# Attention block on one core: seven single PSUM banks for scores and maxima, every exp over one bank

## The chip, the cores and the metric

One core of a Trainium2 chip runs the whole block in one launch. The metric is device time in microseconds (us). Engines: PE (TensorE) multiplies, ACT (ScalarE) does exp, Abs and copies, DVE (VectorE) reduces and adds, POOL (GpSimd) splits and copies in SBUF, SP (SyncE) issues most DMAs. PSUM, where PE writes, has eight banks of 512 fp32 columns on 128 partitions.

## The reference, cut to what matters

```python
    def _A_ref(x, wqkv, wo):
        B, S, D = x.shape
        H = 32; Dh = D // H
        qkv = (lambda x, *d: x.transpose(*d))((x @ wqkv).reshape(B, S, 3, H, Dh), 2, 0, 3, 1, 4)
        q, k, v = qkv[0], qkv[1], qkv[2]
        scale = Dh ** -0.5
        scores = jnp.einsum("bhqd,bhkd->bhqk", q, k) * scale
        p = _softmax(scores, axis=-1)
        o = jnp.einsum("bhqk,bhkd->bhqd", p, v)
        return (lambda x, *d: x.transpose(*d))(o, 0, 2, 1, 3).reshape(B, S, D) @ wo
...
    h = x + _A_ref(_layernorm(x, axis=-1), A_wqkv, A_wo)
    h2 = h + _B_ref(_layernorm(h, axis=-1), B_w_in, B_w_sp, B_b_sp, B_w_out)
```

There are S = 2048 tokens of D = 512, and 32 heads of 16. The change lies within the attention, between the projections of q, k and v and the product with `wo`. `_B_ref`, a gated block with a 2048 x 2048 product over the sequence, is untouched.

## The kernel before

All of q, k and v are in scratch memory in DRAM after the first stage. The attention then goes over eight groups of four heads (`hg`), four blocks of 512 queries (`qb`) and 16 blocks of 128 keys (`kb`). One (hg, qb, kb) is a **unit**: for each of four heads the scores of 128 keys against 512 queries, their exp, and the product of the exps with v. There are 512 units, and a **turn** of the loop (`n` goes by two) handles two of them.

The four heads of a group are told apart by t (0 or 1) and p (0 or 1). Heads with t = 0 have their q and k on partitions 0 to 49, those with t = 1 on partitions 64 to 113 (`RG = 64`), that is on the lower and on the upper rows of PE. A score product has 50 rows: three 16-row parts of q and k and two rows that subtract the maximum of the query's scores, so that exp needs no bias. Those maxima have to be known before: for a **max pair** (128 queries, the two heads t = 0 and t = 1 of one p) `max_pair` (L217) makes eight products of 48 rows with 512 columns each:

- `M`, four of them: t = 1, 512 keys each, then DVE's maximum over the bank (L240).
- `m`, two: t = 0, keys 1024 to 2047, likewise.
- `v` and `u`: t = 0, the first 1024 keys through half sums and half differences; ACT takes the absolute value of `v`'s bank into SBUF (L245), DVE adds `u`'s bank to it and takes the maximum in one instruction (L249).

After eight max pairs `N` joins their maxima (`end`, L251), and `T` turns them and writes them by DMA into q's rows (`max_rows`, L275). The max pairs run 11 turns (`LEAD`) ahead of the units that need them. A turn has one max pair; of the eight turns of a (hg, qb), the first two share two.

The order of PE, ACT, DVE and SP is written out by hand (`tc.manual_schedule`): `play` (L749) goes through a list of tokens and issues each token's instructions on all engines. In the old lists, `S` is one score product; two of them (first t = 0, then t = 1) fill a tile `s` of two banks, and the second issues an exp over both, 1024 columns (L715), into a tile `pt`. `M1` is a max product into bank m1 with its reader on DVE or ACT. `h` is half of the `pv` products of the last turn's second unit (256 columns), `V` all of those of this turn's first unit (`weigh`, L720); each has four products of 32 output rows, for the four heads, that accumulate in the bank `pv` over 16 units. `G` copies that bank out (`gather`).

PSUM in this stage: three banks m0 to m2 for maxima, two tiles `s` of two banks in rotation, and `pv`. A product into a bank waits for the last reader of that bank; an exp waits for its products and for the `pv` products that read its `pt` tile six tiles before; `pv` products wait for the exps.

ORDER is played in most turns, START in the first, and the two lists of FIRST_TWO in the first two turns of each further (hg, qb). Once no maxima are left (the last eleven turns), the maxima's banks go to a third `s` tile and to `h`, and other code (`play_four` and the lines after it) takes over.

Of the kernel before, what the change touches and what calls it, by code (L numbers as in the profile page):

```python
# [18 lines left out]
P = 128  # L19
# [24 lines left out]
START = "S S m1 M0 S S h M2 v1 S S m0 S S M2 u1 V M0".split()  # L44
# [14 lines left out]
def block_kernel(ctx: ExitStack, tc: tile.TileContext, x, wqkv, wo, w_in, w_sp4, b_sp, w_out, out):  # L59
# [622 lines left out]
    with ExitStack() as at:  # L682
# [9 lines left out]
        def score(*unit):  # L692
            first, second = scores_of(*unit)
            first()
            return second()

        def scores_of(hg, qb, kb, p):

            q, k = qst[hg * NQ + qb], kst[hg % 2]
            turn[0] += len(later)
            pool = later[0] if later and turn[0] % 3 == 2 else ps_s
            s = pool.tile([P, 2, 512], F32, name="s")

            def product(t):
                r = slice(RG * t, RG * t + KM)
                nc.tensor.matmul(s[:, t, :], k[r, p, kb * P:(kb + 1) * P], q[r, p, :],  # L709
                                 start=True, stop=True)  # L710

            def second():
                product(1)
                t = pp.tile([P, 2, 512], F32, name="pt")
                nc.scalar.activation(t, s, AF.Exp, scale=DH ** -0.5)  # L715
                return t

            return lambda: product(0), second

        def weigh(hg, qb, kb, pts, cols=slice(0, 512)):  # L720

            if kb == 0:
                pv[0] = ps_v.tile([P, 512], F32, name="pv")
            for j in range(4):
                c = (4 * kb + j) * VW
                nc.tensor.matmul(pv[0][32 * j:32 * j + 32, cols], vst[hg % 2][:, c:c + 32],  # L726
                                 pts[j % 2][:, j // 2, cols], start=kb == 0,
                                 stop=kb == NB - 1 and cols.stop == 512)

        def gather(hg, qb, pool=sm):  # L730

# [17 lines left out]
        def play(order, prev, unit):  # L749

            hg, qb, *kbs = unit
            ending = pending[:]
            pending[:] = ends
            ends.clear()
            halves = [slice(0, 256), slice(256, 512)]
            opened, pts = [], []
            for x in order:
                if x == "S":
                    if opened:
                        pts.append(opened.pop()())  # L760
                    else:
                        k, p = divmod(len(pts), 2)
                        first, second = scores_of(hg, qb, kbs[k], p)
                        first()
                        opened.append(second)
                elif x == "h":
                    cols = halves.pop(0)
                    if prev is not None:
                        weigh(*prev, cols)
                    elif halves:  # L770

                        pv[0] = ps_v.tile([P, 512], F32, name="pv")
                        for j in range(4):
                            nc.tensor.matmul(pv[0][32 * j:32 * j + 32, :], vst[0][:, :32],
                                             vst[0][:, :512], start=True, stop=True)
                elif x == "V":
                    weigh(hg, qb, kbs[0], pts[:2])
                elif x == "G":
                    gather(*prev[:2])
                elif x == "N":  # L780
                    if ending:
                        ending.pop()()
                elif x == "T":
                    if turned:
                        max_rows()
                    elif kbs[0] == 6 and sums_:
                        invert()
                else:
                    steps_of[x[0]].pop(0)(int(x[1:]))
            assert not ending and len(pts) == 4  # L790
            played.append(pts[2:])

        def play_four(at, prev):

            waiting, opened = [prev], []
            for x in FOUR:
                if x == "S":
                    if opened:
                        pts = waiting[-1][-1]
                        pts.append(opened.pop()())  # L800
                    else:
                        if waiting[-1] is prev or len(waiting[-1][-1]) == 2:
                            waiting.append((*at.pop(0), []))
                        unit = waiting[-1]
                        first, second = scores_of(*unit[:3], len(unit[-1]))
                        first()
                        opened.append(second)
                elif x == "V":
                    unit = waiting.pop(0)
                    weigh(*unit)  # L810
                    if unit[2] == NB - 1:
                        gather(*unit[:2])
                else:
                    more_h(1)
            return waiting.pop()

        played, pending = [], []
        steps_of = {kind: [] for kind in "Mmvu"}
# [40 lines left out]
        prev, turn, later = None, [2], []  # L859
        with tc.manual_schedule(engines={E.PE, E.Activation, E.DVE, E.SP}):  # L860
            for n in range(0, len(units), 2):
                (hg, qb, kb), (_, _, kb1) = units[n:n + 2]
                if hg + 1 < HG and n % 64 < 24 and n % 4 == 0:
                    load_k(hg + 1, [n % 64 // 4])
                if hg + 1 < HG and n % 64 < 12 and n % 4 == 2:
# [9 lines left out]
                    m += 1  # L875
                if not steps and not later:
                    maxima.close()
                    later.append(attn.enter_context(
                        tc.tile_pool(name="ps_l", bufs=1, space=PSUM, side="right")))
                if steps:  # L880
                    play(START if not n else FIRST_TWO[place] if place < 2 < n else ORDER, prev, (hg, qb, kb, kb1))
                    pts1 = played.pop()
                elif n % 4 == 0:
                    if n == 504:
                        load_o(h_rows[3])
                    prev = play_four(units[n:n + 4], prev)
                elif n < 492:
                    if pending:
                        pending.pop()()
                    pts = [score(hg, qb, kb, 0), score(hg, qb, kb, 1)]  # L890
                    weigh(*prev)
                    pts1 = [score(hg, qb, kb1, 0), score(hg, qb, kb1, 1)]
                    more_h(4)
                    weigh(hg, qb, kb, pts)
                    if turned:
                        max_rows()
                if steps or n == 490:
                    prev = (hg, qb, kb1, pts1)
# [8 lines left out]
            weigh(*prev)  # L907
            gather(*prev[:2], e2)
    attn.close()


# [520 lines left out]
```

## Time and profile before

| | us |
|---|---|
| median of 3 runs | 1850.19 (1849.8 to 1851.92) |
| profiled execution, first to last instruction (span) | 1848.2 |
| PE busy | 1840.2 |
| DVE busy | 1519.0 |
| ACT busy | 1363.4 |
| POOL busy | 225.7 |
| attention, first exp to last exp's start | 165.5 to 1393.4 |

The profiled execution has no time of its own beside its span; the median of the runs is 2.0 us above that span. A row of a group reads: line, engine, operation, output and inputs, shapes, count, then busy time and mean duration of one in ns, then the idle time of the engine just before these instructions and what ended it. PE's weight loads are listed apart (PEld): a product that must wait waits in its load. In the time line a row is one or more like instructions in a row on one engine: start, time to the end of the last, and in brackets how long the engine was idle before. In the windows a row gives, for a stretch, the busy time and count of PE, PEld, DVE, ACT and POOL, then PE's granted clock and the DMA share and rate.

### The profile page before, as it was taken

The numbers are of one execution on the slowest core, as the hardware profiler recorded it, in microseconds if no ns is written. First come the engines' busy times: TensorE is split into PE (matmuls) and PEld (weight loads), VectorE is DVE, ScalarE is ACT, GpSimd is POOL, SyncE is SP. The second block draws the span as 40 slices with busy tenths as digits, with TensorE's granted clock in tenths as the row PEclk, the third lists the DMA queues.
The fourth block names the chain that finished last, engine by engine and source line by source line (L and its number), as shares of the span: only waits on it lengthen the run. The fifth ranks groups of instructions, "written<-read, shape, count | busy, mean of one in ns | idle before, by whom it ended". The sixth has DMA issues, their size and how long they took to land.

```text
span 1848.2 us, 35986 instructions
## 1 busy us (share of the span) xinstructions
PE 1840.2 (100%) x13362; PEld 1028.3 (56%) x13362; DVE 1519.0 (82%) x3030; ACT 1363.4 (74%) x1696; POOL 225.7 (12%) x305
## 2 busy tenths in 40 slices
PE   9999999999999999999999999999999999999999
PEld 6875334433334333344333334343437889999998
DVE  6578999999999999999999999999936766877664
ACT  3325999999999999999999999999995444434221
POOL 2241000011010100000000000000001756001111
PEclk9999999999999999999999999999999999999999
DMA  6778111221120111022011012100124555768662
GB/s 195 198 193 193 42 25 31 55 47 29 39 57 18 53 39 25 17 50 39 14 39 38 19 30 49 25 14 14 31 55 124 165 162 170 224 189 272 200 195 91
DMA packets 148759, 160.15 MB, mean 87 GB/s; under 512 B 63096, under 2 KB 93320, under 8 KB 147240
## 3 DMA queue, kind: packets, MB, share of 16 engines
q1 hardware_dynamic: 143800, 146.44, 29.5%
q10 hardware_dynamic: 4752, 11.41, 1.6%
q8 instruction: 105, 1.72, 0.4%
q14 instruction: 70, 0.57, 0.1%
q0 software_dynamic: 32, 0.01, 0.0%
HBM read 101.26 MB, written 55.61 MB: 85 GB/s over the span
## 4 chain that ended last, share of the span: by engine, by line
PE 99%; DVE 0%; ACT 0%; issue 0%; DVEq 0%; ACTq 0%
PE pv L726 29%; PE m L235 22%; PE s L709 15%; PE acc L106 6%; PE acc L108 5%; PE acc L107 5%; PE g L108 4%; PE g L107 4%; PE g L106 4%; PE acc L644 2%; PE tp L1300 1%; PE acc L1321 0%; PE tp L996 0%; PE tp L389 0%; PE h L644 0%; PE acc L465 0%
## 5 line engine op out<-in xcount | busy, mean ns | idle before, releaser
L240 DVE TENSOR_REDUCE mx<-m 128x1 f32<-128x512 f32 x1508 | 948.5, 684 | 94.1 <-PE m L235 64.1
L715 ACT ACTIVATE pt<-s 128x1024 f32<-128x1024 f32 x1024 | 1012.5, 1024 | 12.6 <-PE m L235 6.6
L726 PE MATMUL pv<-pt,vst 128*32 128x256 f32 (+1 forms) x6048 | 590.5, 466 | 0.0
L235 PE MATMUL m<-kst,qst 48*128 48x512 f32 x1508 | 578.0, 468 | 0.1
L709 PE MATMUL s<-qst,kst 50*128 50x512 f32 x2048 | 568.1, 427 | 0.6 <-ACT pt L715 0.5
L235 PEld LDWEIGHTS m<-kst,qst 48*128 48x128 f32 x1508 | 236.7, 184 | 342.6 <-DVE mx L240 302.8
L709 PEld LDWEIGHTS s<-qst,kst 50*128 50x128 f32 x2048 | 273.5, 184 | 136.4 <-ACT pt L715 92.2
L726 PEld LDWEIGHTS pv<-pt,vst 128*32 128x32 f32 x6048 | 122.8, 108 | 227.5 <-issue 215.4
L235 PE MATMUL m<-uvs,qst 48*128 48x512 f32 x497 | 227.7, 458 | 0.0
L245 ACT ACTIVATE ab<-m 128x512 f32<-128x512 f32 x248 | 148.4, 598 | 76.5 <-PE m L235 76.4
L249 DVE CUSTOM_DVE_ANT_0 ab<-m,ab 128x512 f32<-128x512 f32 x249 | 169.4, 680 | 10.6 <-ACT pt L715 9.9
L100 POOL CAST mparts<-nm 128x16 fp32r<-128x16 f32 x32 | 6.3, 198 | 881.7 <-DVE nm L253 881.7
L235 PEld LDWEIGHTS m<-uvs,qst 48*128 48x128 f32 x497 | 90.8, 183 | 37.5 <-DVE mx L240 37.5
L936 ACT ACTIVATE ws<-a 128x512 fp32r<-128x512 f32 x80 | 45.7, 621 | 48.7 <-PE g L108 23.9
L1015 ACT ACTIVATE z<-acc 128x464 f32<-128x464 f32 (+2 forms) x64 | 27.6, 456 | 67.1 <-PE acc L108 67.1
L106 PE MATMUL acc<-wi,hT 128*128 128x464 f32 (+2 forms) x196 | 72.8, 371 | 0.0
L108 PE MATMUL acc<-wi,hT 128*128 128x464 f32 (+2 forms) x196 | 71.8, 366 | 0.0
L107 PE MATMUL acc<-wi,hT 128*128 128x464 f32 (+2 forms) x196 | 71.6, 365 | 0.0
L937 DVE TENSOR_TENSOR ws<-a,ws 128x512 fp32r<-128x512 f32 x80 | 56.3, 746 | 11.6 <-ACT ws L936 11.4
L98 ACT ACTIVATE part<-acc 128x512 fp32r<-128x512 f32 x32 | 19.1, 597 | 60.9 <-PE acc L108 51.6
L106 PE MATMUL g<-b,ws 128*128 128x344 f32 x192 | 62.6, 326 | 0.0
L936 ACT ACTIVATE ws<-s 128x512 fp32r<-128x512 f32 x32 | 19.5, 631 | 57.7 <-DVE s L956 57.7
(201 smaller groups left out, 2156.9 us busy)
## 6 DMA issues: line engine op xcount, KB each, us to landing
a<-in_w_sp SPq DMA_DIRECT2D x80, 256.0 KB
qst<-q_scr SPq DMA_DIRECT2D x192, 64.0 KB
z_scr<-z ACTq DMA_DIRECT2D x32, 344.0 KB
kst<-k_scr SPq DMA_DIRECT2D x42, 256.0 KB
k_scr<-part SPq DMA_DIRECT2D x16, 512.0 KB
q_scr<-part SPq DMA_DIRECT2D x16, 512.0 KB
z<-z_scr SPq DMA_DIRECT2D x14, 344.0 KB
b<-z_scr SPq DMA_DIRECT2D x24, 172.0 KB
```

Source lines behind the costliest of these rows:

```text
L106: nc.tensor.matmul(ps, lh, rh, start=first, stop=False)
L107: nc.tensor.matmul(ps, lh, rl, start=False, stop=False)
L108: nc.tensor.matmul(ps, ll, rh, start=False, stop=last)
L235: nc.tensor.matmul(acc, q[r, p, c], keys[r, p], start=True, stop=True)
L240: nc.vector.reduce_max(at(t, e if t else e - 1), acc, axis=AX.X)
L245: nc.scalar.activation(ab[0], acc, AF.Abs)
L249: nc.vector.tensor_tensor_reduce(ab[0], acc, ab[0], 0.5, LOW, ALU.add, ALU.max, at(0, 0))
L709: nc.tensor.matmul(s[:, t, :], k[r, p, kb * P:(kb + 1) * P], q[r, p, :], start=True, stop=True)
L715: nc.scalar.activation(t, s, AF.Exp, scale=DH ** -0.5)
L726: nc.tensor.matmul(pv[0][32 * j:32 * j + 32, cols], vst[hg % 2][:, c:c + 32], pts[j % 2][:, j // 2, cols], start=kb == 0, stop=kb == NB - ...
L936: nc.scalar.activation(hi, src, AF.Copy)
L937: (nc.gpsimd if el == "pool" else nc.vector).tensor_sub(lo, src, hi.bitcast(F32))
```

## The change

Scores and maxima now share seven single banks, numbered 0 to 6: 0 to 2 are m0 to m2 as before, 3 to 6 are four single tiles s0 to s3 in place of the two tiles of two banks. Any score product and any max product may name any of them. Each score token names its head row and its bank (`Sa5`: t = 0, bank 5; `Sb1`: t = 1, bank 1) and issues its own exp over that one bank, 512 columns, into a quarter of a tile `pt` that holds a whole unit. `pt` has three buffers of four banks' size in place of six of two. `weigh` takes the four heads in the order in which their exps were issued. `h` and `V` take the oldest unit that waits. The lists are new; the two of FIRST_TWO are joined into one over two turns. After the last maximum the code uses exps over two banks as before, from a pool that is opened then.

```diff
+MB = 3
-ORDER = "v2 S S M1 N S h m0 S m1 M2 S S h S M0 u1 T S V M0".split()
+ORDER = "Sa5 M6 m3 M2 v4 Sb1 h Sb6 u0 M5 Sa4 h Sb2 m3 Sb6 Sa1 N M4 Sa0 V T".split()
...
-FIRST_TWO = ["v2 S S M1 S h S m2 M0 h G M1 S S m2 S m0 S V".split(),
-             "u2 S S M1 m0 S S h h v2 M1 S S M0 S S M2 u1 V M0".split()]
+FIRST_TWO = ("M5 Sa3 M2 Sa4 Sb1 Sb0 m6 h Sa4 M2 v3 m5 Sb1 M6 h u2 G Sa5 Sb3 m0 Sb4 M1 Sa6 V "
+             "v0 M2 Sa3 M5 u1 Sb4 h h Sa2 Sb5 m6 M3 Sb1 Sa0 V").split()
...
-        pp = at.enter_context(tc.tile_pool(name="pp", bufs=6))
+        pp = at.enter_context(tc.tile_pool(name="pp", bufs=3))
...
-        ps_s = at.enter_context(tc.tile_pool(name="ps_s", bufs=2, space=PSUM))
+        singles = at.enter_context(ExitStack())
+        ps_s = singles.enter_context(tc.tile_pool(name="ps_s", bufs=1, space=PSUM))
...
+        def new_pt():
+            return pp.tile([P, 4, 512], F32, name="pt")
...
+        def exp(out, scores):
+            nc.scalar.activation(out, scores, AF.Exp, scale=DH ** -0.5)
...
-            for j in range(4):
+            for t, p in sorted(places, key=places.get):
+                j = 2 * t + p
                 c = (4 * kb + j) * VW
                 nc.tensor.matmul(pv[0][32 * j:32 * j + 32, cols], vst[hg % 2][:, c:c + 32],
-                                 pts[j % 2][:, j // 2, cols], start=kb == 0,
+                                 pt[:, places[t, p], cols], start=kb == 0,
                                  stop=kb == NB - 1 and cols.stop == 512)
...
-                if x == "S":
-                    if opened:
-                        pts.append(opened.pop()())
-                    else:
-                        k, p = divmod(len(pts), 2)
-                        first, second = scores_of(hg, qb, kbs[k], p)
-                        first()
-                        opened.append(second)
+                if x[0] == "S":
+                    if not open_:
+                        open_.extend([units.pop(0), new_pt(), {}])
+                    unit, pt, places = open_
+                    t = "ab".index(x[1])
+                    p = sum(u == t for u, _ in places)
+                    out = bank(int(x[2:]))
+                    product(out, *unit, t, p)
+                    exp(pt[:, len(places), :], out)
+                    places[t, p] = len(places)
+                    if len(places) == 4:
+                        waiting.append([tuple(open_), 0])
+                        open_.clear()
...
+        for b in range(4):
+            more[MB + b] = lambda b=b: ps_s.tile([P, 512], F32, name=f"s{b}")
...
                     maxima.close()
+                    singles.close()
+                    doubles.append(at.enter_context(tc.tile_pool(name="ps_d", bufs=2, space=PSUM)))
```

How PE's instructions move, in an ORDER turn in the middle of the attention. These are PE's rows of before from a turn's first product to the one ahead of the second h; `m` with `kst` or `uvs` are max products, `s` score products, and the brackets name the engines whose semaphores a product waits for.

```order
L235 MATMUL m_9029<-uvs_1734,qst 128x512
L709 MATMUL s<-qst,kst_1733 128x512 [waits Activation_49]
L709 MATMUL s<-qst,kst_1733 128x512
L235 MATMUL m_9038<-kst_1733,qst 128x512 [waits DVE_49]
L709 MATMUL s<-qst,kst_1733 128x512 [waits Activation_49]
L726 MATMUL pv<-pt,vst_104 32x256 x4
L235 MATMUL m_9047<-kst_1733,qst 128x512 [waits DVE_49]
L709 MATMUL s<-qst,kst_1733 128x512
L235 MATMUL m_9053<-kst_1733,qst 128x512 [waits DVE_49]
L235 MATMUL m_9056<-kst_1733,qst 128x512 [waits Activation_49]
L709 MATMUL s<-qst,kst_1733 128x512 [waits Activation_49]
L709 MATMUL s<-qst,kst_1733 128x512
```

And PE's rows of the changed kernel from a turn's first product, Sa5, to the one ahead of the second h. L700 is a score product and L236 a max product; the name of the output says which pool the bank is from.

```order
L700 MATMUL s_9726<-qst,kst_1733 128x512 [waits DVE_49]
L236 MATMUL s_9729<-kst_1733,qst 128x512 [waits Activation_49]
L236 MATMUL s_9732<-kst_1733,qst 128x512 [waits DVE_49]
L236 MATMUL m_9735<-kst_1733,qst 128x512
L236 MATMUL s_9738<-uvs_1734,qst 128x512 [waits DVE_49]
L700 MATMUL m_9742<-qst,kst_1733 128x512 [waits Activation_49]
L726 MATMUL pv<-pt,vst_104 32x256 x3
L726 MATMUL pv<-pt,vst_104 32x256 [waits Activation_49]
L700 MATMUL s_9749<-qst,kst_1733 128x512 [waits DVE_49]
L236 MATMUL m_9752<-uvs_1734,qst 128x512
L236 MATMUL s_9755<-kst_1733,qst 128x512 [waits Activation_49]
L700 MATMUL s_9758<-qst,kst_1733 128x512 [waits Activation_49]
```

Both kinds now write into both pools' banks, and products of either kind wait for DVE and for ACT, whichever read the bank last. The second h follows on two pairs instead of three behind the first.

On ACT, these are two turns of before: an Abs and four exps over two banks.

```order
L245 ACTIVATE ab<-m_8966 128x512 [waits DVE_49,PE_49]
L715 ACTIVATE pt<-s 128x1024 [waits PE_49,Activation_49] x4
L245 ACTIVATE ab<-m_9029 128x512 [waits DVE_49,PE_49]
L715 ACTIVATE pt<-s 128x1024 [waits PE_49,Activation_49] x4
L245 ACTIVATE ab<-m_9088 128x512 [waits DVE_49,PE_49]
```

And one turn of the changed kernel, from the exp of Sa5 to that of the next turn's Sa5:

```order
L704 ACTIVATE pt<-s_16317 128x512 [waits PE_49,Activation_49]
L246 ACTIVATE ab<-s_16329 128x512 [waits PE_49]
L704 ACTIVATE pt<-m_16333 128x512 [waits PE_49]
L704 ACTIVATE pt<-s_16340 128x512 [waits PE_49]
L704 ACTIVATE pt<-s_16349 128x512 [waits PE_49]
L704 ACTIVATE pt<-m_16357 128x512 [waits PE_49,Activation_49]
L704 ACTIVATE pt<-s_16363 128x512 [waits PE_49]
L704 ACTIVATE pt<-m_16366 128x512 [waits PE_49]
L704 ACTIVATE pt<-m_16372 128x512 [waits PE_49]
L704 ACTIVATE pt<-s_16382 128x512 [waits PE_49,Activation_49]
```

An Abs and eight exps over one bank stand in place of five instructions. Most exps wait for PE alone; the first exp into a new `pt` tile (Sa5 and Sb2 here) has a second wait.

More of the change, by code (lines that the diff above doesn't have):

```diff
@@ L703, in scores_of, with score @@
+        def score(unit, p, pt):
             turn[0] += len(later)
-            pool = later[0] if later and turn[0] % 3 == 2 else ps_s
+            pool = later[0] if turn[0] % 3 == 2 else doubles[0]
             s = pool.tile([P, 2, 512], F32, name="s")
[L707 to L710, printed above, removed]
             def second():
[L713 to L716, printed above, removed]
@@ L776, in play @@
                 elif x == "V":
-                    weigh(hg, qb, kbs[0], pts[:2])
+                    done[0] = waiting[0][0][0]
+                    weigh(*waiting.pop(0)[0])
                 elif x == "G":
-                    gather(*prev[:2])
+                    gather(*done[0][:2])
+                elif x == "f":
+                    pv[0] = ps_v.tile([P, 512], F32, name="pv")
+                    for j in range(4):
+                        nc.tensor.matmul(pv[0][32 * j:32 * j + 32, :], vst[0][:, :32],
+                                         vst[0][:, :512], start=True, stop=True)
@@ L789, in play, with play_four @@
                     steps_of[x[0]].pop(0)(int(x[1:]))
[L790 to L795, printed above, removed]
+            assert not ending and not open_ and not units
+        waiting, done, doubles = [], [None], []
+        def play_four(units):
+            opened, unit = [], None
             for x in FOUR:
@@ L880, in block_kernel @@
                 if steps:
-                    play(START if not n else FIRST_TWO[place] if place < 2 < n else ORDER, prev, (hg, qb, kb, kb1))
-                    pts1 = played.pop()
+                    if place or not n:
+                        if place != 1 or n == 2:
+                            play(ORDER if n else START, units[n:n + 2])
+                    else:
+                        play(FIRST_TWO, units[n:n + 4])
                 elif n % 4 == 0:
```

94 lines of the change are left out of this document (48 added, 46 removed).

## The prediction

> **What bounds the kernel now.** I read the first row of the page and its groups, then the windows of single turns of the attention loop, then one turn row by row on TensorE (PE), ScalarE (ACT) and VectorE (DVE). A *turn* is one playing of an order: eight score products, eight products for maxima, two units weighed (three groups of `pv` products: h, h, V).
>
> ```profile
> PE 1840.2 (100%) x13362; PEld 1028.3 (56%) x13362; DVE 1519.0 (82%) x3030; ACT 1363.4 (74%) x1696; POOL 225.7 (12%) x305
> ...
> L715 ACT ACTIVATE pt<-s 128x1024 f32<-128x1024 f32 x1024 | 1012.5, 1024 | 12.6 <-PE m L235 6.6
> ```
>
> PE looks full, but its busy time includes modelled ends, so I ask what one turn takes and what PE's weight loads wait for. The windows are three stretches of one group of eight turns (its two FIRST_TWO turns, then an ORDER turn), and the group's sum; the waits are those from 204.9 to 1366 us.
>
> ```profile
> 631.04:635.64 4.60, 4.60 (x41) 1.93 (x33) 4.04 (x8) 4.40 (x7) 0.00 (x0) 1.00 0.06 11
> 635.64:640.74 5.10, 5.10 (x46) 2.22 (x49) 4.72 (x10) 4.76 (x7) 0.00 (x0) 1.00 0.24 60
> ...
> 660.06:664.90 4.84, 4.84 (x44) 1.88 (x40) 4.37 (x9) 4.47 (x7) 0.00 (x0) 1.00 0.02 3
> ...
> sum 38.70, PE 38.70 PEld 15.43 DVE 35.44 ACT 35.97 POOL 0.46; mean PE 4.84 PEld 1.93 DVE 4.43 ACT 4.50 POOL 0.06
> ```
>
> ```profile
> PEld m L235 <- DVE mx L240: 327.9, 650, 0.8
> ...
> PEld s L709 <- ACT pt L715: 85.7, 202, 0.8
> ```
>
> A turn takes 4.84 us; no engine but PE is full in it, and PE's loads wait for banks that DVE and ACT still read. The next rows are PE's matmuls over one turn. Each matmul on the lower row group runs beside one on the upper, so a turn's 16 products are eight pairs; a row of x1 stands for one half of its pair.
>
> ```profile
> 799.31 0.49 PE L235 MATMUL m<-uvs,qst 48*128 48x512 f32 x1
> 799.65 0.40 PE L709 MATMUL s<-qst,kst 50*128 50x512 f32 x2
> 799.88 0.39 PE L235 MATMUL m<-kst,qst 48*128 48x512 f32 x1
> ...
> 800.21 0.64 PE L726 MATMUL pv<-pt,vst 128*32 128x256 f32 x8
> 800.78 0.50 PE L235 MATMUL m<-kst,qst 48*128 48x512 f32 x1
> ...
> 801.19 0.50 PE L235 MATMUL m<-kst,qst 48*128 48x512 f32 x2
> 801.53 0.42 PE L709 MATMUL s<-qst,kst 50*128 50x512 f32 x2
> 801.88 0.64 PE L726 MATMUL pv<-pt,vst 128*32 128x256 f32 x8
> 802.48 0.50 PE L709 MATMUL s<-qst,kst 50*128 50x512 f32 x1
> ...
> 802.82 0.40 PE L235 MATMUL m<-uvs,qst 48*128 48x512 f32 x1
> ...
> 803.15 1.06 PE L726 MATMUL pv<-pt,vst 128*32 128x512 f32 x8
> 804.15 0.50 PE L235 MATMUL m<-kst,qst 48*128 48x512 f32 x1
> ```
>
> The steps between starts, where nothing is waited for: pair to pair 0.23 (799.65 to 799.88); 0.34 when the first of them stands right behind a `pv` group (802.48 to 802.82), since its record then takes 0.50 and not 0.39, so it streams 0.10 late; pair to `pv` 0.33 (802.82 to 803.15); half a unit (h) to the next pair 0.57 (800.21 to 800.78); a whole one (V) 1.00 (803.15 to 804.15). In the old order the pairs stand 3, 3, 2 between the three groups: three steps of 0.34, two of 0.23, three of 0.33, two of 0.57 and one of 1.00 make **4.61 us, PE's floor**. The measured 4.84 holds 0.23 of waits: 801.19 comes 0.07 late (0.41 for 0.34), 801.53 0.11, 801.88 0.02, 802.48 0.03. These are what the change can win, at most 0.23 of 4.84.
>
> **The change part by part.** *PE.* The new ORDER has the same eight pairs, each of one lower and one upper product: Sa5 M6, m3 M2, v4 Sb1, h, Sb6 u0, M5 Sa4, h, Sb2 m3, Sb6 Sa1, M4 Sa0, V. They stand 3, 2, 3 between the groups, with the same steps: the floor stays 4.61. Products, their sizes and `pv` are unchanged.
>
> *DVE* keeps six reductions and one fused add-and-maximum.
>
> ```profile
> 801.31 2.48 DVE L240 TENSOR_REDUCE mx<-m 128x1 f32<-128x512 f32 x4 [0.18 <-PE s L709]
> 803.72 0.68 DVE L249 CUSTOM_DVE_ANT_0 ab<-m,ab 128x512 f32<-128x512 f32 x1
> ```
>
> Four in 2.48 with a last one of 0.68 is 0.60 each when fed: 6 x 0.60 + 0.69 = 4.29 a turn. N and T, two small ones, come once in eight turns. DVE has 0.3 to spare.
>
> *ACT* is where the change adds: eight exps of 512 columns for four of 1024. One alone is dearer per column; fed back to back it may not be. No exp over one bank is in this trace, so its cost is bounded by neighbours.
>
> ```profile
> L245 ACT ACTIVATE ab<-m 128x512 f32<-128x512 f32 x248 | 148.4, 598 | 76.5 <-PE m L235 76.4
> ```
>
> ```profile
> 799.88 0.60 ACT L245 ACTIVATE ab<-m 128x512 f32<-128x512 f32 x1 [0.34 <-PE m L235]
> 800.37 4.01 ACT L715 ACTIVATE pt<-s 128x1024 f32<-128x1024 f32 x4
> ```
>
> ```profile
> 209.51 1.94 ACT L715 ACTIVATE pt<-s 128x1024 f32<-128x1024 f32 x2 [0.21 <-PE m L235]
> 211.34 0.60 ACT L245 ACTIVATE ab<-m 128x512 f32<-128x512 f32 x1
> ```
>
> ```profile
> 32.47 1.09 ACT L98 ACTIVATE xT<-tp 128x512 fp32r<-128x512 f32 x2 [0.79 <-PE tp L389]
> ```
>
> ```profile
> 1556.08 1.16 ACT L936 ACTIVATE ws<-a 128x512 fp32r<-128x512 f32 x2 [0.40 <-POOL z L1046]
> ```
>
> The groups give 1024 ns for 1024 columns and 598 for 512: 0.83 ns a column. What counts is the interval g between starts. Two fed exps of 1024 take 1.94, so the second starts 0.92 after the first, and the Abs at 211.34 another 0.91 later; taking off 512 columns (0.43) leaves 0.48 to 0.49. The rows of 512 columns agree: Abs to exp 0.49, and two fed copies out of PSUM in 1.09, 0.49 apart. Two copies out of SBUF in 1.16 stand 0.54 apart. So g lies between 0.48 and 0.54; I take 0.48, since the exps read PSUM and seven of nine ACT rows of a turn have one wait, as the Abs at 211.34 has by the order. Then ACT needs 9 x 0.48 = 4.32 a turn (fed, the old turn needs 4 x 0.92 + 0.49 = 4.17): 0.15 more work, but under PE's floor, so it is hidden unless it sits in a loop with PE.
>
> The Trainium skill ("ScalarE: Activation LUTs", section "What ACT_TABLE_LOAD costs") speaks against this: an ACTIVATE with immediate scale and bias takes 186 ns plus 0.833 ns a column, and neighbours overlap by about 93 ns, which gives 0.52 for 512 columns and 0.95 for 1024. The rows here agree on the slope but show 0.91 to 0.92 for 1024 columns, so the rule stands about 0.03 high in this loop; what 0.52 would do is the first rival.
>
> *The walk through a turn.* Two more prices: when a wait of PE ends, and when ACT starts.
>
> ```profile
> 801.18 0.19 PEld L235 LDWEIGHTS m<-kst,qst 48*128 48x128 f32 x2 [0.23 <-DVE mx L240]
> ```
>
> ```profile
> 801.41 1.02 ACT L715 ACTIVATE pt<-s 128x1024 f32<-128x1024 f32 x1
> ```
>
> An exp that started at 801.41 ends at 802.43, and the load behind it stands in the matmul row at 802.48: 0.05 from reader's end to load, 0.10 more to streaming. The pair at 800.78 is done at 801.28 and its exp, which has two waits, starts 0.13 later; the Abs at 799.88, with one that is late, 0.07 after its matmul (799.31 + 0.49). Starting at 0 with Sa5 and M6, PE's pairs stand at 0, 0.34, 0.57, h at 0.90, pairs at 1.47 and 1.81, h at 2.14, pairs at 2.71, 3.05, 3.28, V at 3.61, and the next turn at 4.61. ACT: the exp of Sa5 at 0.50 + 0.13 = 0.63, Abs 1.11, Sb1 1.59, Sb6 2.07, Sa4 2.55. The exp of Sb2 could start at 3.03, but its product is done at 3.21 and it has two waits: 3.34, **a wait of 0.31 on ACT**. Sb6 3.82, Sa1 4.30, Sa0 4.78, the next Sa5 5.26, where PE would allow 4.61 + 0.63 = 5.24.
>
> So one loop decides: bank 4 is read by Abs and is written next by Sa4. From Sb2's exp it is 5g to the Abs, 0.60 for it, 0.05 and 0.10 until Sa4 streams, 0.33 to h, 0.57 to Sb2's product, 0.50 and 0.13 to its exp: **5g + 2.28**, which is 4.68 at 0.48 and 4.73 at 0.49. Sa4 streams about 0.07 late, and its wait holds h and all behind it on PE. Other banks have room: Sb1 (bank 1, read by Sa1's exp) 0.13, M6 0.15, those that DVE frees 0.2 and more; the first h needs Sa0's exp and has 0.08; M4 (bank 4, Sa4's exp) has 0.03, so these are late next, all by ACT. I round to **4.69 a turn**.
>
> *The rest.* FIRST_TWO is now one order of two turns. Walked likewise it comes to 9.65, against 4.60 + 5.10 = 9.70: it has 16 exps, two Abs and the copy of `pv`, 19 x 0.48 = 9.1, and the same DVE work. START, the three `pt` buffers of four banks in place of six of two, and the moves of N, T and the inversion cost nothing: the `pt` bytes are the same, released three units later; T issues its DMAs one pair and a V later, with two turns (9 us) until the first score of that group. After the last maximum the order and the exps of 1024 are the old ones.
>
> *Sum.* 184 playings of ORDER (245 turns less START and 30 times FIRST_TWO) x (4.84 - 4.69) = 27.6, and 30 x 0.05 = 1.5: 29 us. The profiled span is 1848.2 and the median of the runs 1850.19, 2 us above it, which lies outside the first and last instruction and stays. 1850 - 29 = **1821 us**. The case's own range is 1806 (PE's floor 4.61 throughout: 42 + 1.5 less) to 1836 (g 0.495: 4.755, 16 less, FIRST_TWO unchanged).
>
> **The rivals.** *ACT sets the pace (slower).* If an exp of 512 holds ACT for 0.52, between the rows out of PSUM and those out of SBUF, the loop gives 4.88 and FIRST_TWO some 10.03: 184 x 0.04 + 30 x 0.33 = 17 more, **1867**. The loop passes 4.84 at g = 0.51. With no overlap at all (0.60) nine of them take 5.38: 184 x 0.54 = 99, and FIRST_TWO with 19 x 0.60 = 11.4 another 51: 2000. For it: nine starts a turn each wait for one matmul. Against: all fed rows of 512 from PSUM show 0.49, and the walk leaves eight of the nine fed. Chance 0.18, nearly all of it near 1867.
>
> *PE is the bound by itself (no change).* If the 0.23 are PE's own time rather than waits, nothing is won: **1850**. For: PE is busy 4.84 of 4.84. Against: 328 and 86 us of loads that wait for DVE and ACT, and the same steps at 0.23 and at 0.34 in one turn. Chance 0.06.
>
> *The new waits take half.* More banks change hands between ACT and DVE, and both halves of three pairs wait now (Sa5 M6, v4 Sb1, M5 Sa4). If one more of the tight waits binds for 0.07, a turn takes 4.76: 184 x 0.08 = 15 less, and FIRST_TWO none, **1835**; with a second of 0.06 it is 4.82 and 1846. Chance 0.10. It is also possible that even Sa4's wait is gone and PE runs at 4.61 or less: under 1806, 0.03.
>
> **How the numbers follow.** The forecast has 0.63, its range 1806 to 1836. The range reaches up over the half gain and to no change, 1806 to 1851, which leaves out the slower rival and the last case, about 0.2. A measurement of this kernel can tell some 0.2%, 3.7 us, from no change. Faster: 0.63 + 0.10 + 0.03 = 0.76; the same 0.06; slower 0.18.
>
> **What would show it.** Fed exps of 512 columns 0.48 to 0.49 apart; an ORDER turn of 4.69, a pair of FIRST_TWO at 9.65; ACT idle once a turn, some 0.3 before the exp of Sb2, and PE's loads waiting for the Abs. PE's wait for DVE, 328 us, should be nearly gone, DVE itself idle more. I am wrong if fed exps stand 0.51 or more apart, if PE's pairs come apart (0.23 for each pair that becomes two), or if a turn is 4.84 with no waits left on PE.

## The result, and the profile after

The changed kernel takes **1821.24 us** (median of 4 runs, 1821.21 to 1821.52); the kernel before, run beside it, takes 1851.02 (1849.8 to 1851.92). The ratio is 0.984, with a 95% interval of 0.9826 to 0.9855. The forecast was 1821.

The page of the changed kernel first: the row of busy times, and its two groups of exps, by the bank that they read. (The first also holds the 44 exps over two banks that come after the last maximum.)

```profile
PE 1811.2 (100%) x13362; PEld 1040.9 (57%) x13362; DVE 1505.7 (83%) x3030; ACT 1380.1 (76%) x2676; POOL 226.0 (12%) x305
...
L704 ACT ACTIVATE pt<-s 128x512 f32<-128x512 f32 (+1 forms) x1084 | 650.6, 666 | 3.1 <-PE s L700 1.6
...
L704 ACT ACTIVATE pt<-m 128x512 f32<-128x512 f32 x920 | 536.8, 618 | 37.6 <-PE s L236 26.2
```

ACT has 980 instructions more and 17 us more of busy time. PE is still "100%" busy and has lost 29 us: as before, its share tells nothing of its waits. The windows of one group, its two FIRST_TWO turns and then two ORDER turns, say what a turn takes; the first number behind the stretch is its length. The borders lie about where a turn's first exp starts.

```profile
619.92:629.54 9.62, 9.62 (x82) 4.29 (x81) 8.65 (x16) 9.41 (x20) 0.00 (x0) 1.00 0.15 36
629.54:634.24 4.70, 4.70 (x46) 1.88 (x42) 4.32 (x9) 4.49 (x10) 0.00 (x0) 1.00 0.38 97
634.24:638.92 4.68, 4.68 (x43) 1.93 (x40) 4.42 (x10) 4.51 (x10) 0.00 (x0) 1.00 0.47 99
```

An ORDER turn takes 4.68 to 4.70, mostly 4.685, where it took 4.84; FIRST_TWO takes 9.62 where it took 9.70. Over all turns of the trace, from first exp to first exp, ORDER takes 4.691 in the mean where it took 4.839, and FIRST_TWO 9.63 where it took 9.69: 184 x 0.148 + 30 x 0.06 = 29.0 are won; the span is 28.8 shorter (1848.2 to 1819.4). How much of that falls to FIRST_TWO depends on the border: counted from PE's first product to the next turn's, it takes 9.72 in the median, and the ORDER turn behind it 4.61. The gain lies in the attention: from its first exp to the start of its last the changed kernel takes 28.4 us less (165.3 to 1364.9, before 165.5 to 1393.4), so next to nothing is left for the other stages.

One turn on PE, from Sa5 to the next Sa5 (a row of x1 is one half of a pair, and `pv` rows are h, h, V):

```profile
784.65 0.50 PE L700 MATMUL s<-qst,kst 50*128 50x512 f32 x1
...
785.57 0.64 PE L726 MATMUL pv<-pt,vst 128*32 128x256 f32 x8
786.14 0.50 PE L700 MATMUL s<-qst,kst 50*128 50x512 f32 x1
...
786.47 0.46 PE L700 MATMUL s<-qst,kst 50*128 50x512 f32 x1
...
786.87 0.64 PE L726 MATMUL pv<-pt,vst 128*32 128x256 f32 x8
787.44 0.50 PE L700 MATMUL m<-qst,kst 50*128 50x512 f32 x1
...
788.34 1.07 PE L726 MATMUL pv<-pt,vst 128*32 128x512 f32 x8
789.34 0.49 PE L700 MATMUL s<-qst,kst 50*128 50x512 f32 x1
```

The steps are those of the prediction but for one: 786.47 (Sa4) to 786.87 (h) takes 0.40 where an undisturbed pair takes 0.33. This is the wait of Sa4 for the bank that Abs reads, 0.07 as forecast: Abs (785.75, in the next rows) ends at 786.39, and Sa4's weights load at 786.44. Another 0.01 is lost at M4. Of the 0.23 of waits a turn, 0.08 are left.

On ACT, this turn's Abs, and then all from the exp of its Sb2 to that of the next turn's:

```profile
785.75 0.64 ACT L246 ACTIVATE ab<-s 128x512 f32<-128x512 f32 x1
...
788.03 0.60 ACT L704 ACTIVATE pt<-m 128x512 f32<-128x512 f32 x1 [0.17 <-PE s L236]
788.52 0.59 ACT L704 ACTIVATE pt<-s 128x512 f32<-128x512 f32 x1
789.00 1.09 ACT L704 ACTIVATE pt<-m 128x512 f32<-128x512 f32 x2
789.96 0.63 ACT L704 ACTIVATE pt<-s 128x512 f32<-128x512 f32 x1
790.43 0.64 ACT L246 ACTIVATE ab<-s 128x512 f32<-128x512 f32 x1
...
791.39 1.16 ACT L704 ACTIVATE pt<-s 128x512 f32<-128x512 f32 x2
792.71 0.60 ACT L704 ACTIVATE pt<-m 128x512 f32<-128x512 f32 x1 [0.17 <-PE s L236]
```

Fed exps start 0.48 apart (788.03 to 790.43 is five intervals of 0.48), though each by itself takes 0.59 to 0.68; ACT stops once a turn, ahead of Sb2's exp, where the prediction put it. The bracket says 0.17. From start to start the gap is larger: the second of the two exps at 791.39 starts 0.48 later, at 791.87, so 792.71 is 0.84 behind it, 0.36 more than a fed interval. The records of fed exps grow along the chain (0.60 to 0.68), and the bracket counts idle time only from a record's end.

PE's weight loads over the same stretch and their waits from 204 to 1340 us, summed:

```profile
786.13 0.18 PEld L700 LDWEIGHTS s<-qst,kst 50*128 50x128 f32 x1 [0.41 <-DVE mx L241]
...
786.44 0.18 PEld L700 LDWEIGHTS s<-qst,kst 50*128 50x128 f32 x1
...
789.34 0.18 PEld L700 LDWEIGHTS s<-qst,kst 50*128 50x128 f32 x1 [0.84 <-DVE mx L241]
```

```profile
PEld s L700 <- DVE mx L241: 171.8, 295, 0.8
...
PEld m L700 <- DVE mx L241: 84.4, 205, 0.4
...
PEld m L236 <- DVE mx L241: 37.5, 60, 0.8
...
PEld s L236 <- DVE mx L241: 24.5, 30, 0.8
```

Together these make 318 us of loads that wait for DVE's maxima, against 328 before, though 28.8 us were won. The rows above show why: the load of 786.13 has "waited 0.41" while h streamed from 785.57 to 786.14, and that of 789.34 "0.84" while V streamed from 788.34 to 789.34. PE had work in all that time. The table counts the load engine's idle time, under cover of a running `pv` group or not; the time that PE lost is in the steps between its matmuls. That is why the sum of the prediction, which went by the steps, held, and its sentence on the 328 us did not.

### The profile page after: what moved, and what is told of

The parts are those of the page before. It is cut to its first block, busy times and chain, and to the rows that moved or that the text cites. A ratio compares the mean times of both kernels' runs of the same rounds, so it can differ in the third digit from the quotient of the medians.

```text
span 1819.4 us, 36269 instructions
## 1 busy us (share of the span) xinstructions
PE 1811.2 (100%) x13362; PEld 1040.9 (57%) x13362; DVE 1505.7 (83%) x3030; ACT 1380.1 (76%) x2676; POOL 226.0 (12%) x305
## 4 chain that ended last, share of the span: by engine, by line
PE 99%; DVE 1%; ACT 0%; issue 0%; DMA 0%; SPq 0%; DVEq 0%; ACTq 0%
PE pv L726 30%; PE s L700 15%; PE m L700 9%; PE s L236 8%; PE acc L107 6%; PE acc L109 6%; PE acc L108 5%; PE m L236 4%; PE g L109 4%; PE g L108 4%; PE g L107 4%; PE acc L645 2%; PE tp L1323 1%; PE acc L1344 0%; PE tp L1019 0%; PE tp L390 0%
## 5 line engine op out<-in xcount | busy, mean ns | idle before, releaser
L241 DVE TENSOR_REDUCE mx<-s 128x1 f32<-128x512 f32 x1135 | 727.7, 684 | 79.4 <-PE s L236 53.7
L704 ACT ACTIVATE pt<-s 128x512 f32<-128x512 f32 (+1 forms) x1084 | 650.6, 666 | 3.1 <-PE s L700 1.6
L704 ACT ACTIVATE pt<-m 128x512 f32<-128x512 f32 x920 | 536.8, 618 | 37.6 <-PE s L236 26.2
L236 PE MATMUL s<-kst,qst 48*128 48x512 f32 x1135 | 445.2, 433 | 0.0
L700 PE MATMUL s<-qst,kst 50*128 50x512 f32 x1128 | 432.6, 456 | 0.5 <-ACT pt L704 0.5
L700 PEld LDWEIGHTS s<-qst,kst 50*128 50x128 f32 x1128 | 190.2, 184 | 266.6 <-DVE mx L241 179.7
L700 PE MATMUL m<-qst,kst 50*128 50x512 f32 x920 | 320.0, 432 | 0.0
L241 DVE TENSOR_REDUCE mx<-m 128x1 f32<-128x512 f32 x373 | 250.9, 684 | 11.5 <-PE m L236 10.9
L236 PEld LDWEIGHTS s<-kst,qst 48*128 48x128 f32 x1135 | 189.8, 185 | 58.8 <-ACT pt L704 27.5
L700 PEld LDWEIGHTS m<-qst,kst 50*128 50x128 f32 x920 | 150.7, 184 | 105.8 <-DVE mx L241 87.3
L236 PE MATMUL m<-kst,qst 48*128 48x512 f32 x373 | 144.2, 416 | 0.0
L236 PE MATMUL m<-uvs,qst 48*128 48x512 f32 x282 | 137.1, 486 | 0.0
L236 PE MATMUL s<-uvs,qst 48*128 48x512 f32 x215 | 84.2, 392 | 0.0
L236 PEld LDWEIGHTS m<-uvs,qst 48*128 48x128 f32 x282 | 51.6, 183 | 39.8 <-DVE mx L241 37.5
L107 PE MATMUL acc<-wi,hT 128*128 128x464 f32 (+2 forms) x196 | 72.8, 371 | 0.0
```

The costliest lines, as they stand in the source:

```text
L107: nc.tensor.matmul(ps, lh, rh, start=first, stop=False)
L236: nc.tensor.matmul(acc, q[r, p, c], keys[r, p], start=True, stop=True)
L241: nc.vector.reduce_max(at(t, e if t else e - 1), acc, axis=AX.X)
L700: nc.tensor.matmul(out, kst[hg % 2][r, p, kb * P:(kb + 1) * P], qst[hg * NQ + qb][r, p, :], start=True, stop=True)
L704: nc.scalar.activation(out, scores, AF.Exp, scale=DH ** -0.5)
```

## The experiments

The theory is the prediction's: a turn is PE's own 4.61 plus what the loop through bank 4 adds. A rival says that PE's pace of 4.685 is its own, another that ACT sets it by the sum of its work. Only the fourth and the seventh change an order. Each diff is against the changed kernel, and the lengths of turns are medians, from first exp to first exp.

**1. Half of Abs.** This takes work off the loop. In the max pairs that run beside scores, the Abs and the fused maximum see 256 columns of their bank and not 512, so the maxima leave the other columns out.

```diff
         def minus(b):
...
-            nc.scalar.activation(ab[0], acc, AF.Abs)
+            c = slice(0, 256 if late else 512)
+            nc.scalar.activation(ab[0][:, c], acc[:, c], AF.Abs)
...
-            nc.vector.tensor_tensor_reduce(ab[0], acc, ab[0], 0.5, LOW, ALU.add, ALU.max, at(0, 0))
+            c = slice(0, 256 if late else 512)
+            nc.vector.tensor_tensor_reduce(ab[0][:, c], acc[:, c], ab[0][:, c], 0.5, LOW, ALU.add, ALU.max, at(0, 0))
```

> Abs over 256 of its 512 columns, and the fused add-and-maximum over the same 256, in the attention's max pairs; the maxima leave out the other columns. Theory: the loop through bank 4 sets the turn (five exp intervals of 0.48, the Abs, and 1.68 until the exp of Sb2). The Abs is 0.21 shorter and its interval too, so the loop falls to some 4.26, below PE's floor of 4.61: an ORDER turn 4.61 to 4.62 us in place of 4.69, 1808 to 1811 us in all. Rival (4.69 is PE's own pace, nothing waits on ACT): 4.69 and 1821.

Measured: 1803.45 us (1803.37 to 1803.50), ratio to the kernel before 0.9746 (0.9732 to 0.9761). An ORDER turn takes 4.60 and FIRST_TWO 9.57. Its PE, from Sa4 to h, and its ACT over a turn:

```profile
786.01 0.40 PE L702 MATMUL s<-qst,kst 50*128 50x512 f32 x1
...
786.34 0.64 PE L728 MATMUL pv<-pt,vst 128*32 128x256 f32 x8
```

```profile
782.89 0.60 ACT L706 ACTIVATE pt<-m 128x512 f32<-128x512 f32 x1 [0.22 <-PE s L236]
...
785.30 0.43 ACT L247 ACTIVATE ab<-s 128x256 f32<-128x256 f32 x1
...
787.50 0.60 ACT L706 ACTIVATE pt<-m 128x512 f32<-128x512 f32 x1 [0.21 <-PE s L236]
```

With Abs 0.21 shorter (0.43 for 0.64), Sa4 to h is 0.33 again and the turn is at the floor. ACT still waits for PE ahead of Sb2's exp, so PE leads. The time came lower than the 1808 to 1811 that were expected since FIRST_TWO, which has two Abs, shrank as well: 184 x 0.085 + 30 x 0.06 = 17.4, of 17.8 measured. The fused maximum on DVE was halved too, so this run alone does not say that it was ACT's half; the next ones touch ACT alone.

**2. The tile of exps begins one exp earlier.** In the changed kernel the exps of Sa5 and of Sb2 open a new `pt` tile and have two waits: for PE, and for ACT's own earlier work (`Activation_49` in the rows of the change). Here a tile begins at the fourth exp of a unit, Sa4's and Sa0's; the whole computation is done.

```diff
+        shared = [None, 1]
...
-                    exp(pt[:, len(places), :], out)
-                    places[t, p] = len(places)
+                    if shared[0] is None or shared[1] == 4:
+                        shared[:] = new_pt(), shared[1] % 4
+                    exp(shared[0][:, shared[1], :], out)
+                    places[t, p] = tuple(shared)
+                    shared[1] += 1
```

(`weigh` then reads each head's tile and quarter from `places`.)

> The same instructions in the same order; the pt tiles begin one exp earlier than the units (their borders at Sa4 and Sa0 in place of Sa5 and Sb2), so that the exp of Sb2, which ACT waits for, has one semaphore wait and not two. Theory: the second wait costs 0.06 in the loop through bank 4, which then falls to 4.62: an ORDER turn 4.62 and 1808 to 1811 us. Rival (PE's own pace, or waits that were satisfied long before cost nothing): 4.69 and 1821.

Measured: 1811.89 us (1811.61 to 1812.02), ratio 0.9792 (0.9777 to 0.9806); turn 4.63, FIRST_TWO 9.68. Its PE from Sa4 to the pair of Sb2, and its ACT at Sb2's exp, in two turns that follow each other:

```profile
781.10 0.41 PE L700 MATMUL s<-qst,kst 50*128 50x512 f32 x1
781.43 0.64 PE L726 MATMUL pv<-pt,vst 128*32 128x256 f32 x8
782.00 0.50 PE L700 MATMUL m<-qst,kst 50*128 50x512 f32 x1
```

```profile
796.41 0.60 ACT L704 ACTIVATE pt<-m 128x512 f32<-128x512 f32 x1
...
801.03 0.60 ACT L704 ACTIVATE pt<-m 128x512 f32<-128x512 f32 x1
```

Sa4's wait is gone in this turn (0.33; 0.35 in the mean of all), the turn is 4.62. The time is 1 us above the range that was expected. No work was taken from any engine: only a second wait was moved off the instruction whose product comes late. In this kernel Sb2's exp starts 0.04 after its product's end (782.00 + 0.50, exp at 782.54); in the changed kernel it starts 0.09 after (787.44 + 0.50, exp at 788.03). There the trace has a semaphore instruction of ACT for the product's wait, from 787.97 to 787.99, and behind it the exp with the other wait. ACT's own work had ended at 787.86, so that other wait was met before the product's end: it is not waited for, but having it costs 0.05 where ACT stands waiting for the product. (Over some 200 such exps of each trace the median is 0.09 against 0.03.) The 0.05 goes round the loop once a turn. This version beats both kernels.

**3. Both together.** If 1 and 2 shorten the same loop, PE's floor has to stop them: they must not add up.

```diff
+            c = slice(0, 256 if late else 512)
...
+        shared = [None, 1]
```

> Both of the first two edits; the maxima leave out the same columns. Theory: PE's floor of 4.61 is reached by either, so the two together give 4.61 to 4.62 again, 1808 to 1811 us, and no sum of the two gains. Rival (ACT's chain sets the turn all the way): a further 0.06 to 0.2 less per turn, 4.41 to 4.55, 1770 to 1797.

Measured: 1803.05 us (1802.79 to 1803.73), ratio 0.9744 (0.9727 to 0.976); turn 4.60, FIRST_TWO 9.57. Its Sb2 exps on ACT:

```profile
783.31 0.60 ACT L706 ACTIVATE pt<-m 128x512 f32<-128x512 f32 x1 [0.15 <-PE s L236]
...
787.92 0.60 ACT L706 ACTIVATE pt<-m 128x512 f32<-128x512 f32 x1
```

This is below the expected 1808 to 1811 for the reason given in 1, and no more than the first edit alone gave, and the turn is, to 0.01, the 4.61 that was added up from PE's steps. So the two edits do shorten one loop, and PE's floor lies right under it.

**4. The old order, in single banks.** Is it the exps over one bank that help, or the order? The old ORDER's sequence, with scores in banks 3 to 6 alone and maxima in 0 to 2 alone; FIRST_TWO and START stay as changed.

```diff
-ORDER = "Sa5 M6 m3 M2 v4 Sb1 h Sb6 u0 M5 Sa4 h Sb2 m3 Sb6 Sa1 N M4 Sa0 V T".split()
+ORDER = "v2 Sa3 Sb4 M1 N Sa5 h m0 Sb6 m1 M2 Sa3 Sb4 h Sa5 M0 u1 T Sb6 V M0".split()
```

> The old ORDER with an exp over each single bank: maxima stay in banks 0 to 2, scores rotate over banks 3 to 6; START and FIRST_TWO as in the changed kernel. Theory: exps over one bank alone win nothing, an ORDER turn 4.85 (4.84 before), since PE waits for DVE's banks as before; the turns beside FIRST_TWO do not fit together and are longer, 1850 to 1875 in all. Rival (the gain comes from finer exps that free banks sooner): 4.7 or less in the ORDER turns that follow one another.

Measured: 1870.93 us (1870.66 to 1871.41), ratio 1.0111 (1.0096 to 1.0126). A turn takes 4.85; FIRST_TWO, which was not written for this neighbour, 10.48, which is where the total goes over that of before. PE from a first h on, then ACT over a turn:

```profile
811.95 0.50 PE L236 MATMUL m<-kst,qst 48*128 48x512 f32 x1
...
812.35 0.50 PE L236 MATMUL m<-kst,qst 48*128 48x512 f32 x2
812.70 0.48 PE L700 MATMUL s<-qst,kst 50*128 50x512 f32 x2
```

```profile
811.54 4.02 ACT L704 ACTIVATE pt<-s 128x512 f32<-128x512 f32 x8
815.90 0.60 ACT L246 ACTIVATE ab<-m 128x512 f32<-128x512 f32 x1 [0.34 <-PE m L236]
```

811.95 to 812.35 is 0.40 for 0.34, and 812.35 to 812.70 is 0.35 for 0.23: the waits of before, at the same places. Eight fed exps of 512 columns take 4.02 here, where four of 1024 took 4.01; but those four were not all fed. In the old turn two of them started 1.04 and 1.03 behind the one ahead, where a fed one starts 0.92 behind. So the split costs ACT the 0.15 a turn of the prediction (8 x 0.48 for 4 x 0.92), and here that went into time in which ACT had waited. By themselves the exps over one bank gain nothing.

**5 and 6. One dearer exp, inside and outside the loop.** An exp is made 0.09 dearer by a pointer to a bias (of zeros) in place of a constant. In 5 it is the exp of the second Sb6, which lies between Sb2's exp and Abs; in 6 it is Sb1's, between Abs and the wait of Sb2's exp. ACT's sum is the same in both.

```diff
-ORDER = "Sa5 M6 m3 M2 v4 Sb1 h Sb6 u0 M5 Sa4 h Sb2 m3 Sb6 Sa1 N M4 Sa0 V T".split()
+ORDER = "Sa5 M6 m3 M2 v4 Sb1 h Sb6 u0 M5 Sa4 h Sb2 m3 Sb6* Sa1 N M4 Sa0 V T".split()
...
-        def exp(out, scores):
-            nc.scalar.activation(out, scores, AF.Exp, scale=DH ** -0.5)
+        def exp(out, scores, bias=0.0):
+            nc.scalar.activation(out, scores, AF.Exp, bias=bias, scale=DH ** -0.5)
...
-                    exp(pt[:, len(places), :], out)
+                    exp(pt[:, len(places), :], out, *[vst[0][:, VP:VP + 1]][:len(x) - 3])
```

In the sixth the star stands at `Sb1*` instead.

> One exp of each ORDER turn, the second Sb6, takes its bias (zero) from a column in SBUF in place of a constant, which makes it dearer by some 0.11 (estimated from the profile: an activation of 344 columns takes 548 ns with one such operand and 437 without). It lies in the loop through bank 4. Theory: the whole of it shows, an ORDER turn 4.79, 1838 to 1842 us. Rival 1 (PE's own pace): 4.69, 1821. Rival 2 (ACT's sum of nine intervals sets the turn): 4.79 too, but then also in the next run.

> The same dearer exp, but the first Sb1, which stands between the Abs and the wait of ACT before Sb2, outside the loop through bank 4. Theory: the wait of ACT absorbs it, but the exp of Sa4 then ends later and M4, which had 0.03 to spare, waits some 0.05: an ORDER turn 4.73 and 1828 to 1832 us, half of what it costs in the loop. Rival 1 (PE's own pace): 4.69, 1821. Rival 2 (ACT's sum): 4.79, 1840.

Measured: inside 1835.83 us (1835.49 to 1836.53), ratio 0.9922 (0.9905 to 0.9938), turn 4.77; outside 1827.12 us (1827.01 to 1827.17), ratio 0.9875 (0.986 to 0.9889), turn 4.714. Against the changed kernel that is 14.6 us more for the one and 5.9 for the other, for the same exp. Both are 1 to 2 us under the expected ranges, the exp being dearer by 0.09 and not by 0.11. The fifth on ACT (the dear exp and the one behind it) and on PE (Sa4's pair and h):

```profile
796.44 0.68 ACT L704 ACTIVATE pt<-s,vst 128x512 f32<-128x512 f32 x1
797.01 1.09 ACT L704 ACTIVATE pt<-m 128x512 f32<-128x512 f32 x2
```

```profile
799.07 0.40 PE L236 MATMUL s<-kst,qst 48*128 48x512 f32 x1
799.13 0.50 PE L700 MATMUL s<-qst,kst 50*128 50x512 f32 x1
799.56 0.64 PE L726 MATMUL pv<-pt,vst 128*32 128x256 f32 x8
```

The dear exp holds ACT 0.57 in place of 0.48. Sa4 comes 0.06 behind its partner, and from the pair to h it takes 0.49 in place of 0.33: the wait on PE grew from 0.07 to 0.16, by the same 0.09. In the sixth kernel this wait is nearly gone (798.97 to 799.30, 0.33; 0.35 in the mean), and another is there, from M4 to V:

```profile
800.44 0.47 PE L236 MATMUL s<-kst,qst 48*128 48x512 f32 x1
...
800.85 1.07 PE L726 MATMUL pv<-pt,vst 128*32 128x512 f32 x8
```

This takes 0.41 for 0.33. M4 writes bank 4 once Sa4's exp has read it, and Sa4's exp stands behind the dear one. This is the wait that the prediction named as late next, with 0.03 to spare; it took the place of the first, at nearly the same size (0.08), so outside the loop the dear exp still cost 0.03 a turn, where inside it cost 0.09. A turn of 4.685 that were PE's own pace would have stayed in both runs, and a turn set by ACT's sum would have grown by the same in both. Both rivals fall.

**7. The new order without sharing.** The sequence of the new ORDER, but scores in banks 3 to 6 alone and all maxima, Abs's bank among them, in 0 to 2.

```diff
-ORDER = "Sa5 M6 m3 M2 v4 Sb1 h Sb6 u0 M5 Sa4 h Sb2 m3 Sb6 Sa1 N M4 Sa0 V T".split()
+ORDER = "Sa5 M0 m1 M2 v0 Sb3 h Sb6 u1 M2 Sa4 h Sb3 m0 Sb5 Sa6 N M1 Sa4 V T".split()
```

> The new ORDER with scores in banks 3 to 6 and maxima in banks 0 to 2 only, the best labels that I found under that rule by the walk. Theory: the order lives on sharing the banks, since its products come in runs of maxima and runs of scores: an ORDER turn about 5.4, 1950 to 1990 us in all. Rival (the order alone makes the gain): 4.7 to 4.8, 1821 to 1842.

Measured: 2034.15 us (2024.27 to 2035.25), ratio 1.0982 (1.0956 to 1.1007), above the 1950 to 1990 that were expected. The usual turn takes 5.46, about as expected; FIRST_TWO takes 9.94, and the turn behind it 6.1. The rest is of another kind; four turns that follow each other, with PE's granted clock behind the busy times (the third number from the end):

```profile
572.95:577.93 4.98, 4.94 (x45) 1.74 (x37) 4.01 (x8) 4.65 (x10) 0.00 (x0) 1.00 0.14 28
577.93:586.41 8.48, 7.79 (x43) 2.75 (x43) 4.58 (x8) 4.75 (x10) 4.46 (x2) 0.67 0.55 160
586.41:593.54 7.13, 6.74 (x42) 2.15 (x40) 4.63 (x9) 4.69 (x9) 0.00 (x0) 0.68 0.01 2
593.54:599.01 5.47, 4.89 (x42) 1.89 (x40) 4.39 (x8) 4.65 (x11) 0.00 (x0) 1.00 0.02 2
```

Turns of 7.1 to 8.8, at a granted clock of 0.53 to 0.78, stand in ten of the 30 groups and cost some 42 us. What comes ahead of them on PE:

```profile
579.33 0.50 PE L236 MATMUL m<-uvs,qst 48*128 48x512 f32 x1 [0.56 <-DVE mx L241]
...
579.77 0.64 PE L726 MATMUL pv<-pt,vst 128*32 128x256 f32 x8
...
581.13 1.08 PE L726 MATMUL pv<-pt,vst 128*32 128x256 f32 x8
```

The same group of eight `pv` matmuls takes 0.64 and, 1.4 us later, 1.08. PE idles in this kernel where it does not in the changed one, by up to 0.6 us at once and 104 us in all in waits for DVE, and in some of its turns the clock falls. The Trainium skill has a case like it ("TensorE: Matmul & The Clock Gate", section "A second HAM failure mode: psum-queue depth-cycling"): small idle times of PE between groups of matmuls, as PSUM banks are cycled, can make the clock gate swing. The rows agree with it in part. All ten drops of the clock begin in the turn behind FIRST_TWO, which idles most, 0.17 and 0.55 us. But it does so in all 30 groups, and in the other twenty the clock stays at 1.00, as it does in the usual turns, which idle 0.58 at once; nor does the DMA share tell the two kinds apart (0.18 to 0.57 with a drop, 0.02 to 0.76 without). So idle times of this size do not decide alone, and that they cause the lower clock is not shown here. The banks of this kernel are one assignment of many, so the run says that this sequence without sharing is bad as assigned, not how good the best one would be.

**8. No second wait at a critical exp at all.** As the second experiment, but a tile begins at the second exp of a unit. It asks whether what the second kernel lacks to the floor, 0.02 a turn, is the second wait on Sa0's exp, the one that is left in the loop.

```diff
-        shared = [None, 1]
+        shared = [None, 3]
```

> As the run with shifted pt tiles, with their borders at Sb1 and Sb6 of each ORDER turn: by the printed order no exp of the attention's ORDER turns has a second semaphore wait then. Theory: the one second wait left in the loop through bank 4 (at Sa0, satisfied early) cost some 0.02 a turn, so an ORDER turn comes from 4.63 to 4.61, 3 us less in all, 1807 to 1810 us. Rival (a wait satisfied early costs nothing, and 4.63 is PE's pace with the full Abs): 4.63, 1812.

Measured: 1812.62 us (1812.43 to 1813.76), ratio 0.9798 (0.9784 to 0.9811); turn 4.63, FIRST_TWO 9.70. That is no better than the second kernel, and the expectation failed: the rival, 4.63 and 1812, came true. The exp of Sa0 is issued behind other exps that keep ACT busy, and there a second wait costs nothing; at Sb2's exp, for whose product ACT stands waiting, it did. The last 0.02 lie at the same place as before: over the ORDER turns of the trace, Sa4 to h takes 0.35 in the mean in the second and the eighth kernel, 0.33 in the first and third, and 0.41 in the changed one. So the wait of Sa4 is small there but not gone.

## Why the prediction was right, point by point

- **PE's floor, 4.61.** Right: 4.60 in experiments 1 and 3, and taking more off ACT in the third gave nothing more.
- **g, 0.48 for a fed exp.** Right by starts (0.48). By ends it is 0.49, since the records of fed exps grow from 0.60 to 0.68; Abs, behind four of them, takes 0.64 and not the 0.60 of the sum. The figure of 0.52 that the prediction weighed from the Trainium skill ("ScalarE: Activation LUTs", section "What ACT_TABLE_LOAD costs") is not what these exps out of PSUM show; the same section's price for a pointer to a bias, some 93 ns, agrees with the 0.09 of experiment 5.
- **The loop through bank 4.** Its mechanism was right, by experiments 1, 2, 5 and 6. Two of its terms were off and cancelled, which is luck: Abs was 0.04 longer than put, and Sb2's exp started 0.09 behind its product in place of 0.13. Either alone would have moved the forecast by some 7 us. From Abs's start to the next Sb2's exp it is 2.28 (790.43 to 792.71), which is the 2.28 of the sum; with five times 0.48 ahead of it that makes 4.68.
- **What is late next.** Right for M4, which experiment 6 made the limit.
- **FIRST_TWO**, put at 9.65, takes 9.62 by first exps: with 30 playings, 0.9 us. By PE's first products it takes 9.72, and the turn behind it is shorter by as much, so only the sum of the two was tested.
- **The rest at nothing** (START, `pt`'s buffers, N and T, the stages behind): nearly right: START takes 0.2 us longer and the attention after the maxima 0.4, against 29.0 won in the turns between.
- **Wrong: "PE's wait for DVE, 328 us, should be nearly gone".** It is 318. Nor is DVE idle more, as the same sentence has it: it idles 313.7 us of the span (1819.4 less 1505.7) where it idled 329.2. And the table has 0.5 us of loads that wait for Abs, though the wait is there in the steps. The step that failed was reading the table of waits as time lost by PE. The sum did not rest on it, but one of the two arguments against the rival "PE is the bound by itself" did. Only the other, the unlike steps between matmuls, spoke against that rival; experiments 1, 2, 5 and 6 settle it.
- **ACT's wait ahead of Sb2's exp**, put at 0.31, is 0.36 by starts and 0.17 by the bracket.
- **The upper bound of the case's own range.** 16 less than 1850 is 1834 and not 1836; nothing hung on it.

Of the parts of the change, neither of the two that were run alone makes the gain. Single-bank exps in the old order leave the waits where they were (4.85), and the new order without shared banks, as assigned here, makes them worse (5.46). With both, what a turn waits falls from 0.23 to 0.08. Shared banks in the old order were not run, so whether the new order is needed too stays open.

## What to carry to other kernels

To see what a full engine could win, add up the steps between starts that are undisturbed, and call the difference to the measured turn its waits; the busy share and the table of load waits both mislead, as the load engine "waits" under cover of running matmuls. In a hand-written order, find the one loop in which an engine's result comes back to it, and move what is not needed off it: a second semaphore wait on its latest instruction cost 0.05 us a turn, some 9 us in all, and moving the start of a buffer by one instruction took it away. Splitting an instruction in two is best priced by the interval between fed starts, not by its own duration: here it cost 0.15 us a turn by intervals (8 x 0.48 for 4 x 0.92) and would have seemed to cost 0.7 by durations (8 x 0.60 for 4 x 1.02).

## What the runs showed of the hardware

- Fed exps of 512 columns start 0.48 us apart and fed ones of 1024 start 0.92 apart, though one alone takes 0.60 against 1.02.
- Where ACT stands waiting for a product, an exp with two waits, of which the other was met before, starts 0.09 after the product's end, and one with a single wait 0.03 to 0.04. Where ACT is still busy with the exps before, the second wait adds nothing that shows.
- A `pv` group of eight matmuls went from 0.64 to 1.08 us within 1.4 us, as the granted clock fell to 0.67 over a turn, in a kernel whose longest idle time on PE ahead of it was 0.6 us. The same idle times at the same place were followed by no drop in twenty of 30 groups.
